# Halved first loads on two queues, and three weight parts rounded between the copies of values

## The chip, the cores and the metric

The kernel runs on one core of one Trainium2 chip. The metric is the time of one execution on the device in microseconds. Five engines run their own instruction streams and wait for one another by semaphores: PE (matmul, with weight loads listed apart as PEld), DVE (vector), ACT (scalar and activation functions), POOL (GpSimd) and SP, which here only issues transfers. Transfers are issued on the queues of SP, ACT and POOL; the profile calls them q1, q10 and q0.

## The reference

Two attention layers, A and B, over 2048 tokens, 576 features and 32 heads of 18. Their outputs stand side by side in the result.

```python
# A: one key and value head for all 32 query heads
q = (x @ wq) per head;  k = x @ wk;  v = x @ wv          # k, v: 2048 x 18
p = softmax(q k^T * 18 ** -0.5);  a = (p v, heads joined) @ wo

# B: causal attention inside four segments of 512 tokens, with a memory of the segments before
q, k, v = (x @ wq, x @ wk, x @ wv) per head
g = sigmoid(beta)                                         # one number per head
for s in range(4):
    a_dot = softmax(q_s k_s^T * scale + causal mask) v_s
    a_mem = (phi(q_s) M) / (phi(q_s) z + 1e-6)            # phi(t) = t + 1 if t > 0 else exp(t)
    o_s = g * a_mem + (1 - g) * a_dot
    M += phi(k_s)^T v_s;  z += sum of phi(k_s)
b = (o, heads joined) @ wo
```

## The kernel before

**Precision by parts.** PE takes rounded operands. So each input of a projection is split in two: a high part, which is the value rounded, and a low part, which is the value minus its high part. A projection adds high times high, high times low and low times high. The 576 features are cut in five parts k = 0 to 4: four of 128 rows and one of 64 rows. The last part holds high and low of x in one tile. One projection of 126 columns is thus 14 matmuls (`proj`, L261). Rounding is a CAST on ACT or DVE, the subtraction a TENSOR_TENSOR on DVE or POOL.

**The start.** After twelve matmuls on zeros (L176), A's first chunk of 512 tokens is projected while its parts arrive: for each k, `fillx` makes `xh` (CAST on ACT, L213) and `xl` (DVE, L219), `split_w` makes `wAh` (L230, on DVE for k = 0, else on ACT) and `wAl` (DVE, L231), and PE runs 15 matmuls (L293): five with `xh` and `wAh`, five with `xl` and `wAh`, five with `xh` and `wAl`. The raw parts of x and w of chunk 0 lie in tiles that are used later for B's weights, so these loads show as `wBl`. ACT's table of functions is loaded once ahead of its first CAST.

**A's chunks.** Chunks c = 0 to 3 follow (L272 to L348). In chunk c, while tiles t = 4, 0, 1, 2, 3 are projected, x of the next chunk is prepared. Chunks 0 to 2 of x have places of their own; x(3), A's last chunk, and all chunks of B's x go through the tile `xr`, which has three buffers. Results are split again (`qp`, CAST on ACT, L125, subtraction on DVE, L127) and stored to `qA` and `kA` by SP.

**B's weights.** They come in 15 parts (`WPARTS`): 0 to 9 hold the keys' and values' columns, 10 to 14 the query columns for k = 0 to 4. `load_wpart` (L242) issues a part's transfer on POOL into the tile `wr` (two buffers for parts 10 to 14); part 14 is issued as two halves. `split_wpart` casts it on ACT (`wBh`, L251) and subtracts on POOL (`wBl`, L252). Each of these has its place in its engine's program kept as written (`pin`).

**B's segment 0** (L419 on). Five projections t = 0 to 4 give keys (the fifth holds keys and queries); behind each stand on ACT `qp`, `negative` (L408), the exponential (L414), on DVE the subtraction and phi (L416), and on PE a transpose of phi (`natural`, L432). Then the values, in four groups of 128 tokens and two halves: `values(i, 0)` is 14 matmuls (L513), two copies on ACT (`vch`, L520, and `kn`, L522, the last key head) and a store issued by ACT (L523). `last_key` transposes `kn` for the four groups on PE (L537). Then `values(i, 1)`, then the four query projections with parts 10 to 14. In segment 0 the numbers of `beta` are loaded into `gt` by seven small transfers on POOL (L495), and ACT later takes their exponential (L581).

**What sets the order.** A scheduler orders the instructions of each engine from the program as it is written, by times that it works out itself; `pin` keeps an instruction in its written place. Each engine then runs its list in order. A change in one place can so move instructions elsewhere. Transfers use semaphores in turn, and SP, too, issues its list in order.

**After the projections** come the attention blocks of both layers (L945 to L1002) and the output products, to the end. They are not touched.

Of the kernel before, what the change touches and what calls it, by code (L numbers as in the profile page):

```python
# [22 lines left out]
C = 512  # L23
# [55 lines left out]
def attention_pair_kernel(ctx, tc, a_xT, a_w, a_wo, b_xT, b_w, b_wo, b_beta, ident_d, hmask_d, bmask_d, cmask_d, sel_d, zmask_d, selx_d, sely_d, out):  # L79
# [82 lines left out]
    with ExitStack() as ph:  # L162
# [35 lines left out]
        def load_part(dst, w, c0, n, k, queue):  # L198
            for rows, src in halves(k):
                queue.dma_start(dst[rows], w[src, c0 : c0 + n])  # L200

        def xraw(c, k):
            tile_, c0 = XRAW[c]
            return tile_[:, k, c0 : c0 + C]
# [32 lines left out]
        def load_wpart(i):  # L237
            c0, n, k = WPARTS[i]

            wrs[i] = (p1 if i % 2 and i < 10 else pt).tile([128, 648], F32, name="wr", bufs=2)[:, :n]  # L240
            for rows, src in halves(k):
                pin(nc.gpsimd.dma_start(wrs[i][rows], b_w[src, c0 : c0 + n]))  # L242
# [29 lines left out]
        for c in range(NCH):  # L272
            ready = {}
            if c == 0:

                for k in range(5):
                    load_part(raw[0][:, k, :CA], a_w, 0, CA, k, nc.sync)
                    load_part(xraw(0, k), a_xT, 0, C, k, nc.sync if k else nc.scalar)
                for k in range(5):
                    load_part(xraw(1, k), a_xT, C, C, k, nc.sync)  # L280
                nc.sync.dma_start(ident, ident_d)
                xh, xl, fillx = next_x(a_xT, 0)
                nx = next_x(a_xT, 1)
                for t in TILES:
                    ready[t] = ps.tile([128, C], F32, name="mm", bufs=1) if t == 3 else ps.tile([128, C], F32, name="pj", bufs=4)
                for k in range(5):
                    fillx(k)
                    split_w(wAh, wAl, raw[0][:, k, :CA], 0, CA, k, nc.vector)
                    parts_ = [(wAh, xh), (wAh, xl), (wAl, xh)] if k < 4 else [(wAh, xh), (wAl, xh)]
                    for i, (w, x) in enumerate(parts_):  # L290
                        for t in TILES:
                            M = 114 if t == 4 else 126
                            nc.tensor.matmul(  # L293
                                ready[t][:M],
                                w[:, k, 126 * t : 126 * t + M],
                                x[:, k],
                                start=k == 0 and i == 0,
                                stop=k == 4 and i == 1,
                            )
                for k in range(5):  # L300
                    nx[2](k)
            else:
                xh, xl = nx[:2]
                nx = next_x(a_xT, c + 1) if c < NCH - 1 else next_x(b_xT, 0)
                if c == 2:
                    wBl, wBh = (pw.tile([128, 5, WB], F32R, name=n) for n in ("wBl", "wBh"))
# [112 lines left out]
        for s in range(NSEG):  # L419
# [37 lines left out]
            for t in range(5):  # L457
                if s == t == 0:
                    pj = ahead
                else:  # L460
                    pj = ps.tile([128, C], F32, name="pj", bufs=4)
                    proj(pj[:126], wBh, wBl, xh, xl, 630 + 126 * t if t < 4 else 504, 126)
                if t and not last:
                    natural(f, pkN[:, t - 1, :, 0:126], 0, 126)

                hold = pin
                e = []
                between = (lambda: None) if last and t < 4 else lambda: e.append(negative(pj[:126], 126, hold))
                qp = split2(pt, pj[:126], 126, hold, between)
                if t < 4:  # L470
                    store_parts(qp, 0, 126, kB[s], 7 * t, 7)
                else:
                    store_parts(qp, 0, 72, qB[s], 28, 4)
                    store_parts(qp, 72, 54, kB[s], 28, 3)
                    magnitude(4, pj, pin if last else lambda ins: ins)
                if not last or t == 4:
                    f = phi(pj[:126], 126, "kf" if t < 4 else "qf", 2 if t < 4 else 5, hold, e[0])
                    if t == 4:
                        fs[4] = f
                hold(nc.vector.tensor_reduce(kmB[:126, t : t + 1], pj[:126], axis=AX.X, op=ALU.max, apply_absolute_value=True))  # L480
                if t < 4:
                    hold(nc.vector.tensor_scalar(kbB[:126, t], zmask[:126, t], kmB[:126, t : t + 1], None, op0=ALU.mult))
                if s and not last:
                    nx[2](t, aside=True)
                if s == 0:
                    split_wpart(10 + t)
                    if t < 3:
                        load_wpart(12 + t)
            if s and not last:
                nc.sync.dma_start(qfB[s][: RT[4], 4], fs[4][: RT[4]])  # L490
            if s == 0:
# [36 lines left out]
            if not last:  # L528
                natural(fs[4], pkN[:, 4, :, 0:54], 72, 126)
            for i in range(1, 4):  # L530
                values(i, 0)
            km31 = p2.tile([128, 1], F32, name="km31")

# [1045 lines left out]
```

## Time and profile before

| | us |
|---|---|
| three runs | 1395.25, 1394.51, 1393.42 (median 1394.51) |
| profiled execution, its own time | 1394.57 |
| its span, first to last instruction | 1392.9 |
| PE busy in the span | 1379.1 |
| ACT busy | 1205.8 |
| DVE busy | 1032.6 |
| POOL busy | 260.5 |

Times in the views are from the span's start. A timeline row gives start, duration, engine, line and operation, what is written and read, the count, and in brackets the idle time of that engine just before it and what ended it. A duration of several instructions in one row is that of all of them. Rows of a queue give packets, MB and the share of 16 engines' time.

### The profile page before, as it was taken

The numbers are of one execution on the slowest core, as the hardware profiler recorded it, in microseconds if no ns is written. First come the engines' busy times: TensorE is split into PE (matmuls) and PEld (weight loads), VectorE is DVE, ScalarE is ACT, GpSimd is POOL, SyncE is SP. The second block draws the span as 40 slices with busy tenths as digits, with TensorE's granted clock in tenths as the row PEclk, the third lists the DMA queues.
The fourth block names the chain that finished last, engine by engine and source line by source line (L and its number), as shares of the span: only waits on it lengthen the run. The fifth ranks groups of instructions, "written<-read, shape, count | busy, mean of one in ns | idle before, by whom it ended". The sixth has DMA issues, their size and how long they took to land.

```text
span 1392.9 us, 41210 instructions
## 1 busy us (share of the span) xinstructions
PE 1379.1 (99%) x17455; PEld 835.6 (60%) x17455; DVE 1032.6 (74%) x1509; ACT 1205.8 (87%) x1497; POOL 260.5 (19%) x388
## 2 busy tenths in 40 slices
PE   9999999999999999999999999999999999999998
PEld 6778888755554555555555555555555555555558
DVE  6565463388787887777888877876878778887884
ACT  4543453599999999999999999999999999999992
POOL 2462120012313211312110022113010220001002
PEclk9999999999999999999999999999999999999999
DMA  9876556575564545332322442232103321120023
GB/s 285 261 230 185 180 198 204 188 208 181 153 182 158 147 145 162 101 113 77 105 67 71 141 152 63 85 120 79 52 35 100 104 76 42 31 71 21 18 64 132
DMA packets 88638, 173.67 MB, mean 125 GB/s; under 512 B 12308, under 2 KB 20109, under 8 KB 88018
## 3 DMA queue, kind: packets, MB, share of 16 engines
q1 hardware_dynamic: 81614, 158.91, 36.6%
q0 software_dynamic: 2368, 7.13, 1.8%
q10 hardware_dynamic: 4464, 4.92, 1.1%
q8 instruction: 139, 2.28, 0.7%
q14 instruction: 53, 0.43, 0.1%
HBM read 99.65 MB, written 70.67 MB: 122 GB/s over the span
## 4 chain that ended last, share of the span: by engine, by line
PE 88%; DVE 4%; ACT 3%; DMA 2%; issue 1%; POOL 1%; SPq 0%; DVEq 0%; POOLq 0%; ACTq 0%
PE O L993 33%; PE E L945 20%; PE F L796 11%; PE pj L261 11%; PE E L953 3%; ACT P L963 3%; PE nd L513 2%; DVE W L960 2%; PE pj L513 2%; PE E L1280 2%; PE pj L293 1%; PE F L852 1%; PE F L513 1%; DMA wr<-b_w 1%; DMA vseg<-vB 0%
## 5 line engine op out<-in xcount | busy, mean ns | idle before, releaser
L963 ACT ACTIVATE P<-E 128x1024 f32<-128x1024 f32 (+1 forms) x800 | 783.4, 1066 | 2.0 <-PE E L945 1.6
L960 DVE COPY W<-E 128x1024 f32<-128x1024 f32 (+2 forms) x416 | 453.1, 1089 | 142.2 <-PE E L945 84.1
L993 PE MATMUL O<-P,VA 128*32 128x256 f32 x7504 | 506.8, 379 | 0.0
L963 ACT ACTIVATE P<-W 128x1024 f32<-128x1024 f32 (+1 forms) x330 | 366.8, 1112 | 6.8 <-DVE W L960 6.3
L993 PEld LDWEIGHTS O<-P,VA 128*32 128x32 f32 x7504 | 258.8, 110 | 137.7 <-issue 4.7
L945 PE MATMUL E<-xl,kstA 56*128 56x512 f32 x1920 | 317.3, 430 | 2.1 <-ACT P L963 1.8
L945 PEld LDWEIGHTS E<-xl,kstA 56*128 56x128 f32 x1920 | 155.0, 184 | 159.1 <-issue 94.7
L968 POOL TENSOR_SCALAR_AFFINE_SELECT P<-P 128x256 f32<-128x256 f32 (+1 forms) x192 | 94.6, 493 | 393.4 <-ACT P L963 384.1
L780 POOL TENSOR_TENSOR xh<-xh,rb 126x512 f32<-126x512 f32 (+1 forms) x55 | 70.7, 1308 | 428.7 <-DVE PD L926 185.1
L796 PE MATMUL F<-woB,xh 126*32 126x192 f32 (+1 forms) x1920 | 126.6, 338 | 0.0
L993 PE MATMUL O<-PD,VA 128*32 128x256 f32 x688 | 88.9, 379 | 0.0
L796 PEld LDWEIGHTS F<-woB,xh 126*32 126x32 f32 (+1 forms) x1920 | 38.6, 108 | 74.8 <-issue 69.6
L993 PE MATMUL O<-P,vseg 128*32 128x256 f32 (+2 forms) x1536 | 81.4, 344 | 0.3
L127 DVE TENSOR_TENSOR qp<-pj,qp 126x512 fp32r<-126x512 f32 (+1 forms) x54 | 36.9, 686 | 54.4 <-ACT ph_e L408 32.8
L1002 DVE COPY oe<-O 128x512 f32<-128x512 f32 x64 | 44.2, 691 | 42.6 <-PE O L993 40.8
L261 PE MATMUL pj<-xh,wBh 128*126 128x512 f32 x180 | 72.5, 403 | 0.0
L919 DVE TENSOR_SCALAR PD<-E 128x512 uint32<-128x512 f32 x86 | 59.2, 688 | 16.5 <-PE E L945 14.9
L261 PE MATMUL pj<-xh,wBl 128*126 128x512 f32 x180 | 71.0, 394 | 0.0
L125 ACT CAST qp<-pj 126x512 fp32r<-126x512 f32 (+1 forms) x54 | 31.5, 584 | 42.6 <-PE pj L261 32.6
L993 PEld LDWEIGHTS O<-P,vseg 128*32 128x32 f32 x1536 | 49.1, 110 | 25.3 <-issue 1.8
L796 PE MATMUL F<-woA,xh 126*32 126x192 f32 (+1 forms) x960 | 63.9, 338 | 0.0
L924 DVE SCALAR_TENSOR_TENSOR PD<-PD,n 128x512 f32<-128x512 f32 x86 | 59.5, 692 | 3.0
(238 smaller groups left out, 1570.1 us busy)
## 6 DMA issues: line engine op xcount, KB each, us to landing
stB<-kB SPq DMA_DIRECT2D x96, 144.0 KB
stB<-qB SPq DMA_DIRECT2D x32, 288.0 KB
xl<-qA SPq DMA_DIRECT2D x30, 288.0 KB
oA<-oe SPq DMA_DIRECT2D x32, 256.0 KB
oB<-oe SPq DMA_DIRECT2D x32, 256.0 KB
qA<-qp SPq DMA_DIRECT2D x16, 504.0 KB
kB<-qp SPq DMA_DIRECT2D x16, 504.0 KB
qB<-qp SPq DMA_DIRECT2D x16, 504.0 KB
```

The lines of the kernel that those rows point to most:

```text
L261: hold(nc.tensor.matmul(dst, w[:, c0 : c0 + M], x, start=i == 0, stop=i == len(ops) - 1))
L513: nc.tensor.matmul(pj[:, :n], x, w, start=m == 0, stop=m == len(ops) - 1)
L780: ins = tc.keep_in_program_order(nc.gpsimd.tensor_tensor(dst, a, b, op=op))
L796: nc.tensor.matmul(dst[32 * j : 32 * j + 32], parts[ab, c][: RT[t], t, r0 : r0 + 32], wo[ab][: RT[t], t, c0 : c0 + n], start=start, stop=stop,
L919: v.tensor_scalar(y, e, EXP_A, EXP_B, op0=ALU.mult, op1=ALU.add)
L924: lambda: stt(p, p, POLY[1], u, op0=ALU.add, op1=ALU.mult),
L945: nc.tensor.matmul(e[:, j], kstA[rows, 128 * kt : 128 * kt + 128], st[rows, h, :], start=True, stop=True)
L960: gate.append(nc.vector.tensor_copy(src[:, hs, :n], e[:, hs, :n]))
L963: nc.scalar.activation(p[:, hs, :n], src[:, hs, :n], AF.Exp, scale=SCALE)
L968: nc.gpsimd.affine_select(diag, diag, pattern=[[0, 2], [0, m], [1, 128]], base=0, channel_multiplier=-1, compare_op=ALU.is_ge, fill=0.0)
L993: nc.tensor.matmul(o[32 * j : 32 * j + 32, q0 : q0 + n], v, p[:, j % 2, p0 : p0 + n], start=m == hf == 0, stop=last and hf == 1,)
L1002: nc.vector.tensor_copy(osb, o)
```

## The change

Two edits. First, part 0 of x and of A's weights is loaded in two halves of 64 rows, the upper half by SP's queue and the lower by ACT's, x ahead of the weights on each. Before, x came whole by ACT's queue and the weights whole by SP's. All other first loads stay on SP. Second, the splits of B's query parts 10 to 14, which stood behind the key projections t = 0 to 4 of segment 0, now stand behind t = 1 and t = 3 (parts 10 and 11), and ahead of `values(1, 0)`, `values(2, 0)` and `values(3, 0)` (parts 12, 13, 14). The load of part 12, 13 or 14 follows the split of part 10, 11 or 12.

```diff
             if c == 0:
 
-                for k in range(5):
+                for rows, queue in ((slice(0, 64), nc.sync), (slice(64, 128), nc.scalar)):
+                    queue.dma_start(xraw(0, 0)[rows], a_xT[rows, :C])
+                    queue.dma_start(raw[0][rows, 0, :CA], a_w[rows, :CA])
+                for k in range(1, 5):
                     load_part(raw[0][:, k, :CA], a_w, 0, CA, k, nc.sync)
-                    load_part(xraw(0, k), a_xT, 0, C, k, nc.sync if k else nc.scalar)
+                    load_part(xraw(0, k), a_xT, 0, C, k, nc.sync)
...
                 if s and not last:
                     nx[2](t, aside=True)
-                if s == 0:
-                    split_wpart(10 + t)
-                    if t < 3:
-                        load_wpart(12 + t)
+                if s == 0 and t in (1, 3):
+                    split_wpart(10 + t // 2)
+                    load_wpart(12 + t // 2)
...
             for i in range(1, 4):
+                if s == 0:
+                    split_wpart(11 + i)
+                    if i == 1:
+                        load_wpart(14)
                 values(i, 0)
```

Lines of the changed kernel are 3 to 6 higher than before, from L277 on. PE's list is the same in both. The lists of ACT, POOL, DVE and SP differ, at three places above all.

**ACT at the start**, with the semaphores that an instruction waits for. HW0 and HW1 are those of x's two halves in the change; before, HW0 is that of x. Before:

```order
L200 DMA wBl<-a_xT 128x512
L213 ACT_TABLE_LOAD
L213 CAST xh<-wBl 128x512 [waits DMAHW0_49]
L230 CAST wAh<-wBl 128x618 [waits DMAHW2_49]
L213 CAST xh<-wBl 128x512 [waits DMAHW3_49]
```

In the change:

```order
L277 DMA wBl<-a_xT 64x512
L278 DMA wBl<-a_w 64x618
L213 ACT_TABLE_LOAD [waits DMAHW1_49]
L213 CAST xh<-wBl 128x512 [waits DMAHW0_49]
L230 CAST wAh<-wBl 128x618 [waits DMAHW4_49]
```

The CAST of x now needs two transfers, and the wait for one of them stands on the table load ahead of it.

**SP in A's chunks 1 and 2** (`xr<-a_xT` is x(3), `xr<-b_xT` B's x; one more load of x(3) than shown here, in two halves, stands ahead in both). Before:

```order
L200 DMA xr<-a_xT 128x512 x2
L131 DMA qA_60<-qp 72x1024
...
L131 DMA qA_61<-qp 126x1024 x2
L200 DMA xr<-a_xT 128x512
L131 DMA qA_61<-qp 126x1024 x2
L131 DMA qA_62<-qp 72x1024
L348 DMA kA<-qp 36x1x512
L131 DMA qA_62<-qp 126x1024
L200 DMA xr<-a_xT 128x512
L131 DMA qA_62<-qp 126x1024
L200 DMA xr<-b_xT 64x512 x2
L131 DMA qA_62<-qp 126x1024
```

In the change:

```order
L200 DMA xr<-a_xT 128x512
L131 DMA qA_60<-qp 72x1024
...
L131 DMA qA_61<-qp 126x1024 x2
L200 DMA xr<-a_xT 128x512
L131 DMA qA_61<-qp 126x1024 x2
L131 DMA qA_62<-qp 72x1024
L351 DMA kA<-qp 36x1x512
L131 DMA qA_62<-qp 126x1024
L200 DMA xr<-a_xT 128x512
L131 DMA qA_62<-qp 126x1024
L200 DMA xr<-a_xT 128x512
L200 DMA xr<-b_xT 64x512
```

Of the four whole parts of x(3), two stood ahead of the first store before and one does now; each of the other three has moved back by one place, and the last of them stands behind one more store of q.

**ACT and POOL at segment 0's values.** ACT before (the casts `wBh<-wr` are the splits), behind the fifth projection's `qp`:

```order
L438 ACTIVATE aq<-pj 72x512
L414 ACTIVATE ph_e<-ph_e 126x512
L251 CAST wBh<-wr 128x504
L520 COPY vch<-nd 128x16x18
L522 COPY kn<-nd 128x18
L523 DMA vB_73<-vch 128x304
L520 COPY vch<-nd 128x16x18
...
L522 COPY kn<-nd 128x18
L523 DMA vB_73<-vch 128x304
L547 ACTIVATE ph_1133<-kn 128x72
L581 ACTIVATE gt<-gt 128x7
```

In the change, from the second group's copy:

```order
L251 CAST wBh<-wr 128x504
L522 COPY vch<-nd 128x16x18
L524 COPY kn<-nd 128x18
L525 DMA vB_73<-vch 128x304
L251 CAST wBh<-wr 128x504
L587 ACTIVATE gt<-gt 128x7
L522 COPY vch<-nd 128x16x18
L524 COPY kn<-nd 128x18
L525 DMA vB_73<-vch 128x304
L251 CAST wBh<-wr 128x504
L522 COPY vch<-nd 128x16x18
L524 COPY kn<-nd 128x18
```

And POOL in the change; before, the seven loads of `gt` stood behind the last `wBl<-wr`:

```order
L252 TENSOR_TENSOR wBl<-wr,wBh 128x504
L242 DMA wr<-b_w 128x504
L497 DMA gt<-b_beta 126x1x1 x4
L497 DMA gt<-b_beta 72x1x1
L497 DMA gt<-b_beta 112x1x1
L497 DMA gt<-b_beta 128x1x1
L252 TENSOR_TENSOR wBl<-wr,wBh 128x504
L242 DMA wr<-b_w 64x504 x2
L252 TENSOR_TENSOR wBl<-wr,wBh 128x504 x2
```

The exponential of `gt` has moved up, from behind the fourth copy of `kn` to ahead of the third group's copies, and the loads of `gt` from behind the last split to ahead of part 12's, so that the load of part 14 stands behind them.

## The prediction

> **What bounds the kernel.** I read the page's busy times and chain first, then the windows by stage, then the timeline at the three places that the change touches. From the page, busy times and the chain's shares by engine:
>
> ```profile
> PE 1379.1 (99%) x17455; PEld 835.6 (60%) x17455; DVE 1032.6 (74%) x1509; ACT 1205.8 (87%) x1497; POOL 260.5 (19%) x388
> PE 88%; DVE 4%; ACT 3%; DMA 2%; issue 1%; POOL 1%; SPq 0%; DVEq 0%; POOLq 0%; ACTq 0%
> ```
>
> From the windows: after the stretch its length, busy time of PE, weight loads, DVE, ACT and POOL, the granted clock, DMA share and GB/s.
>
> ```profile
> 57.10:77.00 19.90, 19.90 (x89) 15.68 (x88) 12.72 (x21) 11.23 (x24) 12.41 (x16) 1.00 0.79 264
> 77.00:100.00 23.00, 21.19 (x128) 16.86 (x127) 18.55 (x35) 12.18 (x23) 13.14 (x22) 1.00 0.78 257
> 100.00:112.50 12.50, 12.50 (x95) 12.21 (x94) 3.04 (x10) 3.57 (x13) 4.58 (x8) 1.00 0.35 77
> 177.00:1392.90 1215.90, 1206.28 (x16423) 695.40 (x16415) 933.23 (x1329) 1124.18 (x1335) 198.84 (x296) 1.00 0.36 110
> ```
>
> PE is the bound from its first projection to the end: 19.90 of 19.90 us and 12.50 of 12.50 in two stages of interest, and 1206 of 1216 after 177 us. Its list of matmuls is the same in the changed kernel. So the time moves by what PE starts earlier and by the waits that go or come on PE, us for us; a wait on another engine counts only where PE runs into it. At a granted clock of 1.00 throughout there is nothing for the throttle to give back. I therefore need three terms: the start, the projection of A's last chunk (57 to 61 us), and segment 0 of B (90 to 108 us).
>
> **Term 1, the start: 0.0 us.** Timeline, the first product:
>
> ```profile
> 1.24 1.28 ACT L213 ACT_TABLE_LOAD   x1 [1.24 <-PEq L1572]
> 5.61 0.62 ACT L213 CAST xh<-wBl 128x512 fp32r<-128x512 f32 x1 [3.09 <-DMA wBl<-a_xT]
> 5.80 0.48 DVE L230 CAST wAh<-wBl 128x618 fp32r<-128x618 f32 x1 [4.72 <-DMA wBl<-a_w]
> ...
> 6.32 0.80 DVE L231 TENSOR_TENSOR wAl<-wBl,wAh 128x618 fp32r<-128x618 f32 x1
> ...
> 6.43 1.16 PE L293 MATMUL pj<-xh,wAh 128*114 128x512 f32 x4 [1.26 <-DVE wAh L230]
> ...
> 7.04 0.68 DVE L219 TENSOR_TENSOR xl<-wBl,xh 128x512 fp32r<-128x512 f32 x1
> ...
> 7.78 1.19 PE L293 MATMUL pj<-xl,wAh 128*114 128x512 f32 x4
> ```
>
> PE runs without a break only from 7.78, when `xl` is there; the 6.43 start has a pause behind it. What counts is that moment. `xl` stands behind `wAh` and `wAl` on DVE, so it follows the landing of w (5.78) by about 2.0. In the change, w and x together are still the first 565 KB on the two queues, so I leave w's landing where it is. x's two halves now go first. Packets moved by each queue up to 3.5 us, and by q10 up to 4.5 us (count, MB, share; q10 is ACT's queue with x alone, q1 is SP's):
>
> ```profile
> q10 hardware_dynamic: 81, 0.17, 20.9%
> q1 hardware_dynamic: 58, 0.14, 20.2%
> ...
> q10 hardware_dynamic: 137, 0.26, 24.7%
> ```
>
> 64 packets, a half of x with one row of x each, are through on q10 before 3.5 and on q1 a little later. Before, x's 128 rows were through at about 4.3 by these counts (56 packets in the last microsecond), and its cast began at 5.61, so 1.3 to 1.4 passes from the last packet to the cast. The halves then land at about 4.7 and 5.0. But ACT's order has a new wait: the table load, which ran at 1.24 in the shadow of the load, now carries the wait for x's second half. It begins at 4.7 and ends at 5.95, the cast at 6.57, PE starts at 6.6 and has its five matmuls done at about 7.8. `xl` is ready at 7.75 either way, so PE's unbroken run begins at 7.8: 0.0. Ends: if w landed 0.5 earlier and the table load were hidden, -0.5; if the halves land no earlier than 5.55, table load to 6.85, cast to 7.47, five matmuls to 8.65, +0.9. The other parts of x and w are queued later by up to 1.3 us; part 3's cast at 10.9 feeds matmuls at 16.9, which covers it.
>
> The row of 1.28 us has a page beside it: the Trainium skill, "ScalarE: Activation LUTs", section on what ACT_TABLE_LOAD costs, gives about 1283 ns for the load, which the row confirms, and a further 1380 ns of drain for a switch, which no row here can show, since 3.09 us of idle time follow the load. With that drain between load and cast this term would be about +1.1 instead of 0.0.
>
> **Term 2, x for A's last chunk: +1.9 us.** Rows of SP, DVE and PE:
>
> ```profile
> 42.08 0.38 SPq L200 DMA_DIRECT2D xr<-a_xT  x1
> ...
> 50.11 0.38 SPq L200 DMA_DIRECT2D xr<-a_xT  x1
> 52.61 0.44 SPq L131 DMA_DIRECT2D qA<-qp  x1
> 53.11 2.00 SPq L200 DMA_DIRECT2D xr<-b_xT  x2
> ```
>
> ```profile
> 46.65 1.54 DVE L213 CAST xh<-xr 128x512 fp32r<-128x512 f32 x1
> ...
> 57.10 0.80 DVE L213 CAST xh<-xr 128x512 fp32r<-128x512 f32 x1 [4.51 <-DMA xr<-a_xT]
> ...
> 58.42 0.67 DVE L219 TENSOR_TENSOR xl<-xr,xh 128x512 fp32r<-128x512 f32 x1
> ...
> 60.81 0.43 DVE L213 CAST xh<-xr 128x512 fp32r<-128x512 f32 x1 [1.72 <-DMA xr<-b_xT]
> ```
>
> ```profile
> 59.41 0.39 PE L261 MATMUL pj<-xl,wAh 128*114 128x512 f32 x1
> ```
>
> In this stage part 3 of x(3) was the closest call of the program: issued at 50.11, landed at 57.05, `xl` ready at 59.09, used at 59.41, a slack of 0.3. The order of the changed kernel moves it back by one place. Part 1, which was among the four x(3) loads at about 18 us, now takes the place of part 2 (42.08), part 2 that of part 3 (50.11), and part 3 goes behind the next store of q, which waits for DVE's work and was issued at 52.61. So part 3 is issued at about 53.1, where B's x stood. With the same 6.94 us it lands at 60.05; cast 0.43, `xl` 0.68 and small steps make it ready at 61.25, and PE's matmul of 59.41 runs at 61.3: +1.9. Part 2 in part 3's old place costs 0.4 within that. Ends: with the latency of the 42.08 load, at most 4.57, part 3 is there at 57.7 and DVE comes to it only after 59.09, ready 60.2, +0.8; if it lands as late as B's x did (60.8), +2.6. Behind it on SP stand the loads of B's x, needed from 74 us on with some 3 us to spare, so I put nothing on them.
>
> **Term 3, B's segment 0: +2.6 us net.** ACT and PE, then POOL:
>
> ```profile
> 91.53 0.63 ACT L414 ACTIVATE ph_e<-ph_e 126x512 f32<-126x512 f32 x1
> 94.79 0.61 ACT L251 CAST wBh<-wr 128x504 fp32r<-128x504 f32 x1 [2.63 <-DMA wr<-b_w]
> 95.31 0.58 ACT L125 CAST qp<-pj 126x512 fp32r<-126x512 f32 x1
> ...
> 104.17 0.40 ACT L520 COPY vch<-nd 128x288 f32<-128x288 f32 x1 [1.50 <-PE nd L513]
> 104.47 0.18 ACT L522 COPY kn<-nd 128x18 f32<-128x18 f32 x1
> ...
> 109.80 0.21 ACT L581 ACTIVATE gt<-gt 128x7 f32<-128x7 f32 x1 [4.55 <-DMA gt<-b_beta]
> ```
>
> ```profile
> 93.17 0.40 PE L261 MATMUL pj<-xh,wBl 128*126 128x512 f32 x1
> ...
> 99.12 0.62 PE L432 MATMUL tr<-ident,qf 126*128 126x126 f32 x4 [1.61 <-DVE qf L416]
> ...
> 104.74 0.27 PE L537 MATMUL tr<-ident,kn 128*18 128x128 f32 x1
> ```
>
> What goes: the cast of part 13 waited for its transfer until 94.79, and `qp` of the fifth projection behind it, though PE had finished that at 93.57. With no cast there `qp` starts at 93.6; the 3.81 us from `qp` to PE's transposes (95.31 to 99.12) then end at 97.4, and PE arrives at 97.5. The wait of 1.61 is gone.
>
> What comes: three casts between the copies of values, and behind POOL's new order.
>
> ```profile
> 92.17 1.05 POOL L242 DMA_DIRECT2D wr<-b_w  x2 [0.29 <-POOL wBl L252]
> 98.99 1.26 POOL L252 TENSOR_TENSOR wBl<-wr,wBh 128x504 fp32r<-128x504 f32 x1 [2.23 <-ACT wBh L251]
> 100.19 4.38 POOL L495 DMA_DIRECT2D gt<-b_beta  x7
> ```
>
> ```profile
> DMA to landing us min/median/max: 3.8/5.6/7.3
> wr<-b_w POOLq DMA_DIRECT2D x2, 126.0 KB, 5.2
> DMA to landing us min/median/max: 4.2/5.8/6.2
> ```
>
> (The last three: all loads of `wr`; the two halves of part 14; the loads of `gt`.) I follow POOL and ACT on the old clock of PE. The fourth key part's exponential ended at 92.16, 0.5 of it owed to a cast that is gone: 91.65. Cast of part 11, 0.61: 92.25. POOL's subtraction 1.27, a gap of 0.3, the issue of part 13: 94.4. The seven loads of `gt`, 4.38 us, are now next: POOL is held until 98.8, the last one is issued at 98.15 and lands 5.8 later at 103.95. Then part 12's subtraction: 100.1; only behind it the halves of part 14 are issued, at 100.4 and 100.9, landing at 106.1. On ACT the exponential of `gt` now stands ahead of the third copy of values and waits until 103.95, where before it waited at 109.80 behind the last `kn` with nobody on PE waiting; the third `kn` is done at about 104.7. The cast of part 14 stands ahead of the fourth copy: 106.1 to 106.75, copy and `kn` 0.48, 107.2. PE's fourth transpose of `kn`, at 104.74 before and ready for 103.1 now, runs at 107.3. Against 104.74 that is +2.6, the 1.6 gained already in it (PE's new stall is 4.2 in two pieces). Ends: landing after 3.8 gives 104.7 and +1.2; after 7.3 it gives 108.2 and +4.7. Behind ACT's late copies, `vch` of the second half and the q projections at 112.5 need nothing before 109; part 14's subtraction ends at 108.1 for a use at about 115.
>
> **The sum.** 0.0 + 1.9 + 2.6 = +4.5 us, on the profiled execution's 1394.57 (span 1392.9 and 1.7 around it), which is the median 1394.51 within 0.1: **1399.0 us**, 0.32% slower. Its own range from the ends is 1396 to 1403.
>
> **Rivals.** (a) x's part 3 lands in time after all: less is in the queues at 50 us, since 256 KB moved back. Against it: the 0.3 us of slack and 3 us of later issue. Only term 3 is left: 1397.1, just the same within 0.2%. (b) ACT isn't held, because `gt` and part 14 land early enough for the copies; for it, DMA is at a share of 0.35 after 100 us; against it, seven issues in POOL's line of work. Term 3 is then -1.6: 1394.8. (c) Neither wait is met and the change does what it was cut for, the removed wait alone: not slower, 1392.9. It is decided by part 2 landing before 56.1 and part 3 before 58.2, so that DVE has both `xl` done by 59.4, and by `gt` and part 14 landing before 102; at these places no row shows latencies so short. (d) The halves of x land no earlier than the whole did, and the table load is added in full: +0.9 on the forecast, 1399.9. Beside (d): the Trainium skill, "DMA: Bandwidth & Descriptors", rules for kernel authors, says of two transfers to disjoint partition halves "Don't bother — they serialize", and advises one transfer of 128 partitions; by that rule term 1 is +0.9. The rows agree that both queues share the engines, but they also show x moving from the start on both.
>
> **Chances.** Forecast 0.55, (a) 0.12, (b) 0.12, (c) 0.09, (d) 0.12. Taking 0.2% (2.8 us) as what a measurement here can tell from no change: slower is most of the forecast (0.48), all of (d) and a third of (a), 0.64; the rest, with (b) and nearly all of (c), is the same, 0.33; faster would need more than (c) gives, 0.03. The range is 1394.5 to 1401.5: it leaves out (c) and the top of term 3.
>
> **What would show it.** Right: PE idle of 1 to 2 us before a matmul of `xl` near 60 us, released by DVE; none before the transposes of `qf`; two PE waits on ACT's `kn` near 103 to 107; ACT idle for `gt` and `wr` between the copies; the table load at about 4.7. Wrong: PE's busy share whole from 57 to 77, or the fourth transpose of `kn` no more than 1 us behind the end of the third group of values.

## The result, and the profile after

| | before | changed |
|---|---|---|
| five runs, median (lowest to highest), us | 1394.51 (1393.42 to 1395.25) | 1402.75 (1400.35 to 1405.17) |
| ratio to before, 95% interval | | 1.0061 (1.0047 to 1.0074) |
| profiled execution: its time, span | 1394.57, 1392.9 | 1400.35, 1398.7 |

The changed kernel is 0.6% slower. The forecast, 1399.0, had the direction, but the time lies above the range (1394.5 to 1401.5). The profiled execution is also the fastest of the five, so its trace accounts for 5.8 us and not for the 8.2 of the median; a second trace, below, shows the rest.

From the page of the changed kernel, the busy times, and then three of the four windows that the prediction showed of before (length, busy times of PE, weight loads, DVE, ACT, POOL, granted clock, DMA share, GB/s):

```profile
PE 1382.2 (99%) x17455; PEld 837.0 (60%) x17455; DVE 1032.1 (74%) x1509; ACT 1206.0 (86%) x1497; POOL 261.5 (19%) x388
```

```profile
57.10:77.00 19.90, 18.01 (x77) 13.35 (x76) 14.13 (x23) 9.23 (x20) 11.48 (x14) 1.00 0.76 249
77.00:100.00 23.00, 23.00 (x134) 18.57 (x132) 16.46 (x34) 12.27 (x24) 12.93 (x25) 1.00 0.80 258
100.00:112.50 12.50, 9.27 (x58) 8.30 (x57) 3.15 (x10) 4.36 (x13) 6.45 (x8) 0.88 0.41 109
```

The page alone says nothing: one per cent of 1394 us is 14, and PE is 99% busy in both. The windows say where. From 57 to 77 us PE loses 1.9 of 19.9; from 77 to 100 it gains the 1.8 that it waited before; from 100 to 112.5 it is idle for 3.2, and the granted clock is 0.88 where it was 1.00.

PE's waits up to 130 us, by what they waited for (total, times, longest):

```profile
PE tr L543 <- ACT kn L524: 3.2, 2, 2.5
PE pj L261 <- DVE xh L213: 1.4, 1, 1.4
...
PE pj L296 <- DVE wAh L230: 0.5, 1, 0.5
```

**The start** of the changed kernel, from the timeline (start, duration):

```profile
4.77 1.28 ACT L213 ACT_TABLE_LOAD   x1 [4.77 <-DMA wBl<-a_xT]
6.06 0.62 ACT L213 CAST xh<-wBl 128x512 fp32r<-128x512 f32 x1
...
6.29 0.48 DVE L230 CAST wAh<-wBl 128x618 fp32r<-128x618 f32 x1 [5.21 <-DMA wBl<-a_w]
...
8.27 1.19 PE L296 MATMUL pj<-xl,wAh 128*114 128x512 f32 x4
```

The half of x that the table load waits for landed at 4.77, near the forecast, and the other by 6.06 at the latest, where the cast starts without a further wait. But the weights landed only at 6.27 instead of 5.78. PE's unbroken run begins at 8.27 instead of 7.78.

**x's third part**, from the timelines of SP, DVE and PE:

```profile
53.47 0.42 SPq L200 DMA_DIRECT2D xr<-a_xT  x1
...
61.23 0.43 DVE L213 CAST xh<-xr 128x512 fp32r<-128x512 f32 x1 [1.74 <-DMA xr<-a_xT]
...
61.72 0.48 PE L261 MATMUL pj<-xh,wAh 128*114 128x512 f32 x1 [1.45 <-DVE xh L213]
62.45 0.49 PE L261 MATMUL pj<-xl,wAh 128*114 128x512 f32 x1 [0.24 <-DVE xl L219]
```

Issued at 53.47, landed at 61.2, 7.7 us later. **B's values**, from the timelines of POOL, ACT and PE:

```profile
97.14 4.37 POOL L497 DMA_DIRECT2D gt<-b_beta  x7
101.47 1.34 POOL L252 TENSOR_TENSOR wBl<-wr,wBh 128x504 fp32r<-128x504 f32 x1
103.10 1.11 POOL L242 DMA_DIRECT2D wr<-b_w  x2 [0.29 <-POOL wBl L252]
...
107.24 0.21 ACT L587 ACTIVATE gt<-gt 128x7 f32<-128x7 f32 x1 [4.59 <-DMA wr<-b_w]
108.28 0.61 ACT L251 CAST wBh<-wr 128x504 fp32r<-128x504 f32 x1 [0.47 <-DMA wr<-b_w]
...
107.86 0.28 PE L543 MATMUL tr<-ident,kn 128*18 128x128 f32 x1 [2.49 <-ACT kn L524]
109.32 0.32 PE L543 MATMUL tr<-ident,kn 128*18 128x128 f32 x1 [0.74 <-ACT kn L524]
```

POOL's line of work is the forecast one: seven loads of `gt`, then part 12's subtraction, then part 14's loads, and ACT stuck behind both. The wait of 4.59 us is that of the exponential of `gt`, which reads `gt` and not `wr`: the last three loads of `gt` took 6.3 to 7.1 us from issue to landing. What comes next was not in the forecast. Windows of the changed kernel behind this wait:

```profile
105.50:109.25 3.75, 0.72 (x5) 0.49 (x5) 0.54 (x3) 1.53 (x6) 0.28 (x1) 1.00 0.35 114
109.50:112.75 3.25, 3.25 (x15) 2.96 (x15) 1.88 (x5) 1.10 (x3) 0.72 (x1) 0.50 0.14 48
112.75:114.00 1.25, 1.25 (x11) 1.25 (x10) 0.70 (x2) 0.40 (x1) 0.00 (x0) 0.96 0.24 56
```

After 3.75 us in which PE was busy for 0.72, the granted clock is 0.50 for 3.25 us. PE counts as fully busy there and does half the work: 15 matmuls, where the next 1.25 us hold 11.

**Where the time went, by landmarks.** For a few instructions of PE, the start in the timeline, and how much later than before. "q projection" is the first matmul of B's first query projection.

| start, us (against before) | before | changed | changed, 2nd trace | first edit alone | x halved | second edit, `gt` late | 'mix' |
|---|---|---|---|---|---|---|---|
| first matmul with `xl` | 7.78 | 8.27 (+0.5) | 8.78 (+1.0) | 8.27 (+0.5) | 7.86 (+0.1) | 7.44 (-0.3) | 7.52 (-0.3) |
| A's last transpose of v | 63.67 | 66.79 (+3.1) | 68.63 (+5.0) | 68.27 (+4.6) | 66.89 (+3.2) | 63.31 (-0.4) | 63.39 (-0.3) |
| transposes of `qf` | 99.12 | 100.14 (+1.0) | 101.97 (+2.9) | 102.05 (+2.9) | 101.99 (+2.9) | 96.66 (-2.5) | 97.17 (-2.0) |
| fourth transpose of `kn` | 104.74 | 109.32 (+4.6) | 111.59 (+6.9) | 108.07 (+3.3) | 107.58 (+2.8) | 103.92 (-0.8) | 102.76 (-2.0) |
| q projection | 112.48 | 118.57 (+6.1) | 122.19 (+9.7) | 115.81 (+3.3) | 115.32 (+2.8) | 111.63 (-0.9) | 110.50 (-2.0) |
| span | 1392.9 | 1398.7 (+5.8) | 1402.5 (+9.6) | 1396.1 (+3.2) | 1395.8 (+2.9) | 1392.1 (-0.8) | 1391.2 (-1.7) |

All of it is decided in the first 122 us; what PE is late by then, it is late by at the end, within 0.3.

### The profile page after: what moved, and what is told of

Same layout as the page of the kernel before. It is cut to its first block, busy times and chain, and to the rows that moved or that the text cites. A ratio compares the mean times of both kernels' runs of the same rounds, so it can differ in the third digit from the quotient of the medians.

```text
span 1398.7 us, 41214 instructions
## 1 busy us (share of the span) xinstructions
PE 1382.2 (99%) x17455; PEld 837.0 (60%) x17455; DVE 1032.1 (74%) x1509; ACT 1206.0 (86%) x1497; POOL 261.5 (19%) x388
## 4 chain that ended last, share of the span: by engine, by line
PE 87%; DVE 4%; ACT 4%; DMA 2%; issue 1%; POOL 1%; SPq 0%; DVEq 0%; ACTq 0%; POOLq 0%
PE O L999 32%; PE E L951 20%; PE F L802 11%; PE pj L261 11%; ACT P L969 3%; PE E L959 3%; DVE W L966 2%; PE pj L515 2%; PE nd L515 2%; PE E L1286 2%; PE pj L296 1%; DMA vseg<-vB 1%; DMA xr<-a_xT 1%; PE F L515 1%; DVE sm L751 0%
## 5 line engine op out<-in xcount | busy, mean ns | idle before, releaser
L969 ACT ACTIVATE PD<-W 128x512 f32<-128x512 f32 x86 | 60.9, 708 | 1.1 <-DVE W L966 1.1
```

The costliest lines, as they stand in the source:

```text
L969: nc.scalar.activation(p[:, hs, :n], src[:, hs, :n], AF.Exp, scale=SCALE)
```

## The experiments

The theory: three waits (start, x's third part, values) and, on top, a halved clock behind a wait. The rivals are in the expectations. All times are against runs of before on the same chip: median 1394.13 for 'loads', 'splits', 'splits_gtlate' and 'mix', 1395.22 for 'after_again', 'splits_fill', 'whalf' and 'after_gtlate', 1394.60 for 'after_fill', 'xhalf' and 'mix_again'.

### The first edit alone ('loads')

The first hunk of the diff, and nothing else.

> The first edit alone (first parts in halves, all later parts of x on SP's queue; the query weights rounded as before). Theory 'three waits and a halved clock': only the waits of this edit remain, 0.5 us at the start (w landed at 6.27 instead of 5.78) and 2.6 us at the matmuls of x's third part near 61 us, and a wait of 1.45 us there was followed by no lowered clock in the profiled execution of the changed kernel: before + 3.1 us, about 1397.6, mean clock 1.000 as before. Rival 'loose clock': the lower mean clocks of the changed kernel (0.996 to 0.998) come with the loads' order in some executions, not with the stall at the values: then this kernel too shows 0.996 to 0.998 and a spread of some 4 us, about 1399 to 1402. Rival 'the loads are harmless by themselves': 1394.5, the wait near 61 us being brought on by the second edit.

Measured: 1397.47, ratio 1.0025 (1.0017 to 1.0034). The size came out as the theory said, but for another reason: the clock was not at 1.00. PE's waits there, and the windows around them:

```profile
61.84 0.55 PE L261 MATMUL pj<-xh,wAh 128*114 128x512 f32 x1 [1.56 <-DVE xh L213]
...
63.56 0.63 PE L261 MATMUL pj<-xh,wAh 128*114 128x512 f32 x1
63.99 0.63 PE L261 MATMUL pj<-xh,wAl 128*114 128x512 f32 x1
...
66.09 0.39 PE L261 MATMUL pj<-xh,wAl 128*126 128x512 f32 x1
66.32 0.39 PE L261 MATMUL pj<-xh,wAh 128*126 128x512 f32 x1
```

```profile
60.00:62.00 2.00, 0.44 (x3) 0.16 (x1) 0.61 (x2) 0.00 (x0) 1.70 (x2) 1.00 0.88 305
62.25:65.50 3.25, 3.08 (x8) 2.32 (x8) 0.86 (x2) 0.82 (x2) 0.00 (x0) 0.50 0.95 325
```

Matmuls of 512 columns start 0.43 us apart at a clock of 0.50 and 0.23 apart at 1.00. So a wait of 1.56 us can be followed by a halved clock too, where one of 1.45 in the first trace of the changed kernel was not. The rival 'loose clock' had this right, a lower clock without the stall at the values, but not its time: two of eleven executions lie above 1399. Two more things are in the landmarks. The loss is +4.6 at 64 us and +2.9 at the transposes of `qf`: coming late, PE no longer meets the old wait of 1.61 us, since part 13 is there by then. The first edit thus takes away by its lateness the very wait that the second edit was to remove.

### The second edit alone ('splits')

The second and third hunks of the diff, and nothing else.

> The second edit alone (three roundings between the copies of values; the loads as before). Theory 'three waits and a halved clock': the wait of 1.61 us before the transposes of the fifth features goes, two PE waits on the copies of kn come (2.5 and 0.7 us in the changed kernel), net +1.5 us, and behind them the granted clock is at 0.50 for about 3 us, +1.5 more: about 1397.5, mean clock 0.998, and perhaps the spread of the changed kernel. Rival 'one late, all late': the stall at the values comes from the start's 3.1 us of delay against transfers that keep their time; then PE has no wait there that is over 1 us, the clock stays at 1.000, and the time is 1393 to 1394.5.

Measured: 1400.22, ratio 1.0048 (1.0034 to 1.0061); slower than the theory had it by 2.7. The rival fell: the wait at the values is there without the first edit, and longer. PE's wait and the window behind it:

```profile
107.11 0.38 PE L540 MATMUL tr<-ident,kn 128*18 128x128 f32 x1 [4.21 <-ACT kn L521]
```

```profile
107.50:110.50 3.00, 2.81 (x12) 2.19 (x12) 0.82 (x2) 2.03 (x6) 1.26 (x1) 0.50 0.30 104
```

PE reaches `kn` earlier here and so waits 4.2 us for the same late transfers; the halved clock follows. On ACT the exponential of `gt` starts at 106.48, after 6.31 us of idle time, and the cast of part 14 behind it, at 107.45, waits for no transfer any more. So `gt` is the hold that ended last here; part 14's halves, at 5.3 us from their issues at 101.15 and after, landed at about the same time. The two edits don't add: +3.3 and +6.1 alone, +8.2 together.

### The second edit with the loads of `gt` behind the copies ('splits_gtlate')

```diff
                 nc.vector.memset(gt, 0.0)
-                for t, lo, hi, n in [(t, H0[t], H0[t] + HT[t], DH) for t in range(5)] + [(5, 0, 28, 4), (6, 28, 32, 32)]:
-                    pin(
-                        nc.gpsimd.dma_start(
...
                 values(i, 0)
+            if s == 0:
+                for t, lo, hi, n in [(t, H0[t], H0[t] + HT[t], DH) for t in range(5)] + [(5, 0, 28, 4), (6, 28, 32, 32)]:
+                    pin(
+                        nc.gpsimd.dma_start(
...
```

> The second edit alone, with the seven loads of the gate's factors issued behind the copies of values, so that POOL reaches part 12's subtraction and part 14's loads without them. Theory 'POOL's line': the third copy of kn is then in time, part 14 is issued about 0.9 us earlier and still lands late (5 us of transfer behind a subtraction that itself waits for a rounding behind the first copy), so one PE wait of 2 to 3 us is left, before the fourth transpose of kn; 1.0 us better than the second edit alone, about 1396.5 with the halved clock and 1395.0 without it. Whether the clock halves behind one wait of that length is open; the profile tells. Rival 'the transfer is slow because of the loads around it': without the seven loads in the queues part 14 lands in 4 us or less and no wait over 1.5 us is left: 1393.5 to 1394.5.

Measured: 1393.82, ratio 1.0002 (0.9994 to 1.0011): 6.4 us better than the second edit alone, by a move of seven transfers of at most half a KB. The theory's wait of 2 to 3 us was too long; here the rival was nearer. Part 14, from POOL's and ACT's timelines, and PE's wait:

```profile
98.81 1.05 POOL L242 DMA_DIRECT2D wr<-b_w  x2 [0.29 <-POOL wBl L252]
...
102.88 0.61 ACT L251 CAST wBh<-wr 128x504 fp32r<-128x504 f32 x1 [2.68 <-DMA wr<-b_w]
```

```profile
PE tr L541 <- ACT kn L515: 1.5, 1, 1.5
```

Part 14 is issued 2.3 us earlier than in 'splits' (101.15; PE itself is 1.0 earlier by then), and its halves take 3.4 us to land by the median instead of 5.3, with no small transfers ahead of them in POOL's queue. Whether it is these transfers that lengthened it or the load of the moment was not separated. Nor were the two holds on ACT: the edit takes away the exponential's wait for `gt` ahead of the third copy and the delay of part 14 together, and no run takes away one of them alone. No half-clock stretch follows the 1.5 us.

### The changed kernel, once more ('after_again')

No edit.

> The changed kernel once more, for another profiled execution and the spread of its times. Theory 'waits and a halved clock by chance': the same PE waits at the same places in every execution (about 0.5 at the start, 1.5 near 61 us, 3 to 4.5 at the transposes of kn), and the granted clock at 0.50 for about 3.4 us behind each wait or not, as it falls out; each such stretch costs about 1.6 us. So single times between 1399 and 1405 with mean clocks of 0.999 to 0.996, the median near 1402, and in this profile half-clock windows behind the wait near 61 us, behind the one at 105 to 109 us, or behind both, and nowhere else before 1390 us. Rival 'the transfers vary': the spread comes from longer waits in some executions; then a slow profiled execution shows a PE wait over 5 us at the transposes of kn or over 2.5 us near 61 us, with one half-clock stretch at most.

Measured: 1403.34, ratio 1.0057 (1.0043 to 1.0071); single times 1402.3 to 1404.4. This trace shows what the first had not: half-clock stretches behind both the wait near 61 us and the one at the values. Windows:

```profile
63.50:66.75 3.25, 3.25 (x9) 2.57 (x8) 1.22 (x3) 2.30 (x5) 0.54 (x1) 0.50 0.92 279
66.75:67.50 0.75, 0.75 (x4) 0.56 (x4) 0.75 (x1) 0.00 (x0) 0.75 (x2) 0.88 0.83 306
...
111.25:118.00 6.75, 6.41 (x27) 6.12 (x28) 2.58 (x6) 1.79 (x6) 1.26 (x1) 0.50 0.28 73
```

and its waits:

```profile
PE tr L543 <- ACT kn L524: 3.7, 2, 3.0
PE pj L296 <- DVE wAh L230: 1.4, 1, 1.4
PE pj L261 <- DVE xh L213: 1.3, 1, 1.3
```

The second stretch is twice as long as any other, 6.8 us. The rival (longer waits) fell: the waits are 0.2 shorter near 61 us and 0.5 longer at the values. Of the 3.8 us by which this trace is longer than the first, the landmarks give 0.5 to the start, 1.3 to the stage at 64 us (a shorter wait and a half clock of some 1.6), 0.4 to the values, 1.4 to the stretch behind them.

### Work in PE's wait ('splits_fill' and 'after_fill')

```diff
+                if s == 0:
+                    fill = ps.tile([128, C], F32, name="mm", bufs=1)
                 for i in range(4):
-                    hold(nc.tensor.transpose(tr[:DH, i], kn[:, i], ident))
+                    if s == 0 and i >= 2:
+                        for _ in range(17 if i == 2 else 5):
+                            pin(nc.tensor.matmul(fill, wBh[:, 0, 0:128], xh[:, 0], start=True, stop=True))
+                    (pin if s == 0 else hold)(nc.tensor.transpose(tr[:DH, i], kn[:, i], ident))
```

That is the second edit alone, filled. 'after_fill' is the changed kernel with `matmul(fill, ident, xh[:, 0].bitcast(F32))` in its place, three times and once, and once ahead of x's third part in the projection of A's last chunk.

> The second edit alone, with 17 added matmuls of 512 columns (0.235 us each, 4.0 in all) in PE's wait ahead of the third transpose of kn and 5 (1.2 us) ahead of the fourth; their result is used by nothing, and nothing else waits for them. PE so has work while it waits, and the copies of kn come as late as before. Theory 'the halved clock follows the idle time': the clock stays at 1.000 up to 1390 us; the wait itself still costs what it did (the fourth transpose at about 108.5 us), and three matmuls that ran in it (0.4 us) move behind it; the 1.6 us of the halved clock are saved: about 1.2 us under the second edit alone, 1398 to 1399, and a spread of some 2 us. Rival 'the halved clock has another cause' (the load, or the place in the program): clock 0.997 to 0.998 and 1400.5 as before, or more.

> The changed kernel with five added matmuls of 128x512 on unrounded values (estimated at four times the 0.235 us of a rounded one, 0.9 us each): one in PE's wait near 61 us, three ahead of the third transpose of kn, one ahead of the fourth. Few instructions this time, where the 22 of the earlier filled kernel came with a pause of 2.93 us at 233 us that no other kernel had and that halved the clock there. Theory 'the halved clock follows idle time': no half-clock window between 20 and 200 us; what is left are the waits themselves: start 0.5 to 1.0, near 61 us 2.5, the values net 1.5, and 0.4 for work that moves behind the fill: before + 5.2, about 1399.7, and single times within 2.5 us of one another. Rival 'the halved clock has another cause': two half-clock windows as before, 1403.

Measured: 'splits_fill' 1401.94, ratio 1.0042 (1.0026 to 1.0059); 'after_fill' 1402.66, ratio 1.0054 (1.0041 to 1.0067). By the clock the theory held, by the time it missed. Windows of 'splits_fill', then of 'after_fill':

```profile
102.00:107.00 5.00, 5.00 (x25) 3.95 (x24) 0.54 (x3) 1.59 (x7) 0.92 (x2) 1.00 0.34 108
107.00:110.50 3.50, 3.50 (x26) 2.96 (x25) 2.31 (x6) 1.44 (x4) 0.59 (x1) 1.00 0.13 44
```

```profile
62.00:67.00 5.00, 4.42 (x18) 3.35 (x19) 2.74 (x6) 2.31 (x5) 1.02 (x2) 1.00 0.95 311
109.00:112.75 3.75, 2.97 (x16) 1.90 (x17) 1.31 (x5) 2.10 (x8) 1.26 (x1) 1.00 0.24 83
```

The copies of `kn` come late here too (fourth transpose at 107.21 and 110.55), PE has work meanwhile, and the clock stays at 1.00 behind it: in these two traces it is the idle time that matters, not the place or the load. The time was not saved for two reasons. In both, a pause that names no releaser appears near 236 to 240 us, far behind the edit:

```profile
236.21 0.29 PE L662 MATMUL mm<-vch,pkN 128*32 128x57 f32 x4 [2.93 <-issue]
```

```profile
239.87 0.40 PE L263 MATMUL pj<-xl,wBh 128*126 128x512 f32 x1 [1.17 <-issue]
```

In 'splits_fill' the clock halves behind it: PE is 3.1 us late at the q projection (115.59), and the span is 7.3 longer. Two of its six runs, at 1398.55 and 1398.71, lie where the theory put all of them, and their mean clocks are 0.999 and 1.000, against 0.998 of the three near 1402. The slowest, 1404.21 at 0.999, is not explained. And in 'after_fill' the work that moved behind the fill took 0.9 from the fourth transpose to the q projection (8.66 against 7.74 before), not 0.4. What the pause is stays open. It isn't bound to added PE instructions: 'splits', which has none, has one of 0.69 us ahead of 239.90; of the other traces none has one there. So the cost of a half-clock stretch is told by rows and landmarks (1.5 from 109.32 to 118.57, less the 7.74 of before) and by the mean clocks of single executions (last section), and not by these two medians.

### Which half of the first edit ('whalf', 'xhalf')

```diff
-                for k in range(5):
+                nc.scalar.dma_start(xraw(0, 0), a_xT[0:128, :C])
+                for rows, queue in ((slice(0, 64), nc.sync), (slice(64, 128), nc.scalar)):
+                    queue.dma_start(raw[0][rows, 0, :CA], a_w[rows, :CA])
+                for k in range(1, 5):
```

That is 'whalf'; 'xhalf' halves x in the same way, ahead of whole weights on SP's queue.

> The kernel before with only A's first weight part in halves (upper half by SP's queue, lower by ACT's behind x, which goes whole as before). The orders of SP from the second weight part on, of DVE, of POOL and of ACT behind the two issues are word for word those before: the four loads of x's last chunk stand in their old places, and the table load waits for nothing. Theory 'order of SP': no PE wait over 0.3 us near 61 us, clock 1.000; w lands between 5.5 and 6.3 us, so -0.3 to +0.5 at the start: 1393.8 to 1394.6. Rival 'any halving at the start disturbs the later transfers': a PE wait of 1 us or more near 61 us, 1396 or more.

> The kernel before with only part 0 of x in halves (upper on SP's queue ahead of the whole weight part, lower on ACT's). SP's order is that of the changed kernel: one load of x's last chunk ahead of the first store where there were two, its last part behind one more store of q. Theory 'order of SP': a PE wait of 1.3 to 1.6 us near 61 us (2.5 us by the place of PE), with or without a half-clock window, no such wait at the fifth features at 99 us, since PE comes late there; w lands at 6.0 or later, start +0.2 to +0.5: 1396 to 1398.5. Rival 'it takes the halves of w' (more transfers on ACT's queue): no wait near 61 us, 1394 to 1395.

Measured: 'whalf' 1395.13, ratio 0.9997 (0.9989 to 1.0006); 'xhalf' 1397.70, ratio 1.0025 (1.0016 to 1.0035). The theory held in both for SP's order and for the time. PE has no wait near 61 us in 'whalf'; in 'xhalf', from SP's and PE's timelines:

```profile
53.82 0.38 SPq L200 DMA_DIRECT2D xr<-a_xT  x1
...
59.13 0.49 PE L261 MATMUL pj<-xh,wAh 128*114 128x512 f32 x1 [0.50 <-DVE xh L213]
61.24 0.49 PE L261 MATMUL pj<-xl,wAh 128*114 128x512 f32 x1 [1.62 <-DVE xl L219]
```

The last part of x's last chunk is issued at 53.82 in SP's new order. So the wait near 61 us comes from the order that the scheduler made of loads up to 50 us later, and it made that order for the halves of x, not for those of w. In 'xhalf' the cast of the weights began at 5.44 and the start lost 0.1; in 'whalf' the start lost 0.2. The larger loss, 0.5 and more in every trace of a kernel with both halved, needs both. Two points of the expectation for 'xhalf' missed: the weights were forecast at 6.0 or later, and a wait of 1.0 us at the `qf` transposes was left.

### The changed kernel with the loads of `gt` behind the copies ('after_gtlate')

The edit of 'splits_gtlate', on the changed kernel.

> The changed kernel with the seven loads of the gate's factors issued behind the copies of values. With the second edit alone that took the PE wait at the transposes of kn from 4.4 to 1.5 us. Theory 'the parts add': what is left is the first edit's loss, measured at +3.3 us, and the second edit's -0.3: about 1397.2, and PE waits of about 1.5 us near 61 us and 1 to 2 us at the fourth transpose of kn. Rival 'the late start makes the second wait worse': over 1399.

Measured: 1398.15, ratio 1.0020 (1.0010 to 1.0030), where the changed kernel stands at 1.0057 to 1.0061. The theory that the parts add (1397.2 at a before of 1394.13, so +3.1) held, with +2.9. The place of the seven small transfers in POOL's line and of the exponential that reads them, with the clock that follows, is worth about 5 of the 8 us. Its trace has a surprise at the start, PE's wait and the windows:

```profile
PE pj L296 <- DVE wAh L230: 1.9, 1, 1.9
```

```profile
5.00:7.25 2.25, 0.38 (x3) 0.04 (x1) 0.60 (x2) 1.04 (x3) 0.00 (x0) 1.00 0.96 290
8.00:11.00 3.00, 3.00 (x9) 2.28 (x8) 2.87 (x5) 1.92 (x3) 0.00 (x0) 0.50 1.06 324
```

The first product, too, can pay a half clock: the late weights cost 2.2 us here and not 0.5 (the first matmul with `wAl` starts at 11.19, before at 9.03). One of the ten executions has a mean clock of 1.000 and took 1394.13; the other nine have 0.998 and lie between 1397.48 and 1399.39.

### A version that removes the wait without a new one ('mix', 'mix_again')

Before, with these changes, and the loads of `gt` behind the copies as above:

```diff
-                if s == 0:
+                if s == 0 and t < 3:
                     split_wpart(10 + t)
-                    if t < 3:
-                        load_wpart(12 + t)
+                    load_wpart(12 + t)
...
             for i in range(1, 4):
+                if s == 0 and i < 3:
+                    split_wpart(12 + i)
                 values(i, 0)
```

> The kernel before, with the roundings of parts 10 to 12 and the loads of 12 to 14 one projection earlier than the changed kernel has them (behind the first, second and third projection, as before), those of 13 and 14 ahead of the second and third copies of values, and the seven loads of the gate's factors behind the copies. Theory: the rounding of part 13 no longer stands ahead of the fifth qp, so the wait of 1.61 us goes; parts 13 and 14 were loaded long before their roundings, so no copy of kn is late and the clock stays at 1.000: before - 1.6, about 1392.9. Rival 'nothing is gained': PE runs into the next wait (copies behind a rounding of 0.6 us each, or the gate's factors, used later): 1394 to 1395.

> The kernel of the run 'mix' once more, on another chip perhaps, for a second interval. Theory: before - 1.2 as measured there, the removed wait of 1.61 us being all that it can gain; ratio 0.999, 0.9985 to 0.9997. Rival 'nothing is gained': 1.000.

Measured: 1392.96, ratio 0.9994 (0.9986 to 1.0003), and 1393.90, ratio 0.9995 (0.9986 to 1.0004). The trace is the theory's: ACT's rounding of parts 13 and 14 waits for no transfer, and PE is 2.0 us earlier at the transposes of `kn`:

```profile
97.07 0.61 ACT L251 CAST wBh<-wr 128x504 fp32r<-128x504 f32 x1 [0.41 <-ACT kn L515]
99.12 0.61 ACT L251 CAST wBh<-wr 128x504 fp32r<-128x504 f32 x1 [0.39 <-ACT kn L515]
...
102.76 0.27 PE L539 MATMUL tr<-ident,kn 128*18 128x128 f32 x1
```

Against the changed kernel that is some 9 us. Against before both intervals reach past 1.000 (1.0003 and 1.0004): a gain of some 0.8 us by the ratios, which these measurements don't tell from none.

## Why the prediction was wrong

- **The step that failed** is the sentence in the first part, "At a granted clock of 1.00 throughout there is nothing for the throttle to give back." The clock was at 1.00 while PE had no long idle time; the change makes idle time. The trace of before shows this once itself: from 1389.6 us on, two us behind PE's last matmul, its granted clock is 0.50. The prediction found the new idle time and priced it at its length. In the first trace the half clock costs 1.5 more (from +4.6 to +6.1 between the fourth transpose and the q projection), in the second some 1.6 and 2.9. Without it the first trace would stand at +4.6, against the +4.5 of the sum. That the two agree is luck, since the terms in that sum were partly wrong in ways that cancelled:
- **Term 1, 0.0:** measured +0.5 and +1.0, in one kernel +2.2 with a half clock. The assumption "I leave w's landing where it is" was wrong: w landed at 6.27 and 6.78, before at 5.78. x came earlier and w later, and PE needs both. The table load at 4.77 and the cast behind it were forecast to 0.1 us, and were not on the path. The same rows show no drain: the cast starts at 6.06, the table load ends at 6.05. The Trainium skill, "ScalarE: Activation LUTs", section on what ACT_TABLE_LOAD costs, gives a further 1380 ns of drain for every switch to a different set. No such time stands between this first load and its cast; a switch between sets no run here shows. (By the prediction's own steps such a drain would have made an estimated +1.4 of the term, not +1.1.)
- **Rival (d)** was near the price of the start (+0.9), but had the wrong mechanism: the half of x that was waited for did land earlier. The rule beside it, from the Trainium skill, "DMA: Bandwidth & Descriptors", rules for kernel authors, that halves serialize, agrees with the two together: x came 0.8 earlier, w 0.5 later.
- **Term 2, +1.9:** right in its mechanism, and 'xhalf' and 'whalf' show it to be SP's order; mis-sized in its latency, 7.7 us instead of the 6.94 of before, behind an issue 0.4 later than forecast, so +2.6, the upper end. In one trace the half clock came on top.
- **Term 3, +2.6 net:** right in its mechanism. The gain was larger, 2.1 instead of 1.6 (from +3.1 to +1.0 in the first trace). The stall was smaller, 3.6 instead of 4.2 by the landmarks (from +1.0 to +4.6), of which the two waits are 3.2: net +1.5. But most of the gain isn't the second edit's: in 'loads', PE, late by the first edit, has 1.7 of it anyway (from +4.6 to +2.9).
- **Rivals (a), (b), (c)** fell: part 3 was late, ACT was held by `gt` and by part 14.
- **The range** left out the top of term 3, though the ends of the terms reached 1403, and held no rival in which an idle PE costs more than the idle time. That rival, at +1.5 for each of two waits, would have put 1402 inside.

## What to carry to other kernels

Price a new wait on a busy PE at its length plus a possible 1.5 us or so of half clock behind it, even if the clock stands at 1.00 in the rows of before: they only say that PE was never idle enough within one window of 3.4 us. When an edit moves work on one queue, list what it now stands behind there, however small, on every engine that it touches: seven transfers of at most half a KB, ahead of one needed load on POOL and awaited on ACT ahead of needed copies, were the largest part of this loss. And two edits that each touch a wait must be summed in order, since PE made late by one no longer meets the wait that the other removes.

## What the runs showed of the hardware

- The half clock comes in stretches of one length. Read by windows of 0.25 us, it stands at 0.50 for 3.4 us in six places, and for 6.8, twice that, in one; why it stayed down there is open, since PE was busy for 3.1 of the first 3.4 us. It can start well after the wait: in the second trace of the changed kernel PE's last pause there ended at 62.70, and the clock went down at 63.51.
- The drops lie on a grid of 3.4133 us that runs through the whole execution. The clock also goes down behind PE's last matmul; counting that drop, the changed kernel's first trace has drops at 109.44 and 1396.26, 377 times 3.4133 us apart, and its second at 63.51, 111.30 and 1401.54, 14 and 378 times apart. In the other four traces with more than one drop ('loads', 'splits', 'splits_fill', 'after_gtlate') the distances are whole multiples too, to 0.02 us. For the other traces the grid is taken from the last drop alone. So the wait doesn't start the stretch; a window that runs on its own does. The Trainium skill, "TensorE: Matmul & The Clock Gate", part 1, describes such a free-running window of about 3.4 us, and the rows agree.
- Whether a wait is followed by it isn't told by its length. Of PE's waits between 1.29 and 1.87 us that the traces of these kernels hold, three of eleven were (1.29, 1.56, 1.87), eight not (the longest 1.62, and another of 1.29); of those with 2.49 us or more all three, and the pause of 2.93 us too. It is told nearly by PE's busy time in the window of the grid that holds most of the wait. The clock went down behind every window with PE busy for up to 1.67 of the 3.41 us, behind one of five between 1.80 and 1.88, and behind none with more; the wait of 1.61 us in before lies in one with 1.80. The same part of the page gives one idle window of that length as what halves the clock; here windows in which PE was busy for up to about half of the time were enough, and the measurement decides.
- Much of the spread of single times goes with the clock. Of the eleven executions of 'loads', five with a mean clock of 0.999 took 1396.07 to 1396.81, four with 0.998 took 1397.47 to 1397.90, and two with 0.997 took 1400.44 and 1401.28. Of the changed kernel's first five, the one with 0.998 took 1400.35, the two with 0.997 took 1401.30 and 1402.75, and the two with 0.996 took 1404.10 and 1405.17. One stretch of 3.4 us at half speed takes some 0.001 off the mean. It isn't all of the spread: 'xhalf' has executions of 1400.51 and 1400.63 at 0.999.
